# One product of the first block named behind every short matmul of the attention, in the order named

## The chip, the cores and the metric

The program runs on one NeuronCore of a Trainium2 chip (trn2). The metric is the device time of one execution in microseconds (us), lower is better. The engines are named as in the profile: PE is TensorE's matmuls, PEld its weight loads, DVE VectorE, ACT ScalarE, POOL GpSimd, SP SyncE, whose queue issues DMAs.

## The reference: attention and two blocks

All tensors are f32. Attention: batch 4, 8 heads, 576 positions, head dimension 64, with a mask by blocks of 64. Its output becomes 2304 tokens of 512 values. The first block is `h = max(x@w1, x@w2, x@w3)` (width 768), then `h@w_out` (back to 512). The second block is a sum over four experts: `p[:, e] * (relu(x@w1[e]) @ w2[e])`, width 1024.

```python
scores = scale * np.matmul(q, k.transpose(0, 1, 3, 2))      # masked, softmax, then @ v
h = np.maximum(np.maximum(x @ w1, x @ w2), x @ w3); x = h @ w_out
for e in range(E):
    out += p[:, e:e + 1] * (np.maximum(x @ w1[e], 0.0) @ w2[e])
```

## The kernel before

Precision. Most products run on operands split into a high and a low half (`fp32r`), three matmuls for one f32 product (`mm3`, L544 to 554: high with high, high with low, low with high).

Attention (L611 on) goes head by head, g = 0 to 31, eight heads a batch, two heads a pair. The stages of one head are `turn_probs` (transposes of the probabilities on PE, L323, in banks of four tiles, copied out by ACT at L338 and DVE at L339), `values` (products with v, L396 and L404) and `scores` for the head after next (L254, then DVE's minimum, ACT's exponential at L275). On odd heads the next pair is prepared as well (`prep_pair`; `turn_raw` transposes q and k, L199; the DMAs of L158 and L159 copy q to q on ACT's queue). An odd head takes the stages in the order ta, s0, tb, s1, prep, va, prep, vb; an even one in the order ta, tb, va, vb, s0, s1. The PSUM tiles of all of these come from one pool of four banks (`ps_x`).

The first block of a batch (`moe1`) needs the attention of the whole batch. It is a generator, and so its matmuls (L551: 128 rows by 288 columns) are handed out in bits. One bit is six matmuls, a batch has `UNITS` = 96 of them (576 matmuls). `Filler.upto(n)` hands out bits until n are done. After each stage of heads 8 to 31 the kernel asks for as many as the share of the batch that is through, less `LAG` = 10 bits. So batch 0's block is spread over the attention of batch 1, and so on; that of batch 3 comes after the attention.

```python
at = (g + (n + 1) / len(todo)) / H
filler.upto((at - 1) * UNITS - LAG)
```

Order. The program names instructions in an order; a list scheduler that simulates the engines then writes each engine's queue. Where two instructions don't depend on each other, it may take the one named later first, if its inputs are there sooner. `tc.keep_in_program_order(ins)` forbids that for one instruction: it stays behind the instruction of its engine that was named just before it. It adds no semaphore. In the kernel before, no matmul of attention or of the first block is held so. Each engine then runs its queue strictly in order.

The second block (L839, L901 to 903) runs after all of this and is not touched, except that a bit is now one matmul where its first inputs are made (L924).

Of the kernel before, what the change touches and what calls it, by code (L numbers as in the profile page):

```python
# [11 lines left out]
ALU = mybir.AluOpType  # L12
AX = mybir.AxisListType

LAG = 10

WT = 5

# [1 line left out]
P = 128  # L20
# [5 lines left out]
def program(tc, q, k, v, w1, w2, w3, w_out, probs, e_w1, e_w2, out):  # L26
# [166 lines left out]
    def turn_raw(g, to, half):  # L193

        raw = pairs[g]["raw"]
        for r0, r1 in (((0, 8), (8, 16)), ((16, 18),))[half]:
            t = ps_x.tile([P, 512], F32, name="tq", tag="x")
            for r in range(r0, r1, 2):
                nc.tensor.transpose(  # L199
                    t[:, (r - r0) * 64:(r - r0) * 64 + P], raw[:, r:r + 2].rearrange("p r d -> p (r d)"), ident  # L200
                )
            tv = t.rearrange("x (i h p) -> x i h p", h=2, p=64)
            todo = []
            for odd, own, other in ((0, lo, hi), (1, hi, lo)):
                for n in range(2):
                    rs = [r for r in range(r0 + odd, r1, 2) if r // R == n]
                    if rs:
                        dst = to(n, rs[0] - n * R, rs[-1] - n * R + 1, 2)
                        src = tv[own, (rs[0] - r0) // 2:(rs[-1] - r0) // 2 + 1]
                        todo.append((n, dst[own], dst[other], src))  # L210
            for n, high, low, src in todo:
                nc.scalar.activation(high, src, ACTF.Copy, scale=1.0 if n else -scale)
            for n, high, low, src in todo:
                if n:
                    nc.vector.tensor_tensor(low, src, f(high), op=ALU.subtract)
                    continue
                for h in range(2):
                    nc.vector.scalar_tensor_tensor(
                        low[:, :, h], src[:, :, h], -scale, f(high[:, :, h]), op0=ALU.mult, op1=ALU.subtract
                    )  # L220
# [8 lines left out]
    def scores(g, grp):  # L229
        pair, h = pairs[g // 2], g % 2  # L230
        if grp == 0:
            heads[g] = dict(
                p=[None] * 4,
                mn=ap_.tile([P, 5], F32, name="mn", tag="mn", bufs=3),
                sm=ap_.tile([P, 5], F32, name="sm", tag="sm", bufs=3),
            )
        mn, sm, pt = heads[g]["mn"], heads[g]["sm"], heads[g]["p"]
        c0 = 3 * grp
        sets = []
        for tag, cols, plan in GROUPS[1][h] if grp else GROUPS[0]:  # L240
            st = (ps_x if tag == "x" else ps_c).tile([P, cols], F32, name="st", tag=tag)
            sets.append((st, plan))
            for i, o, w in plan:

                if i == 4:
                    todo = [(QT + 64 * x, x) for x in range(2)]
                else:
                    todo = [(h * QT // 2 + P * i, h)]
                c = 0
                while c < w:  # L250
                    n = min(w - c, 512 - (o + c) % 512)
                    terms = [(part, q0, x) for q0, x in todo for part in ("q1", "q2")]
                    for m, (part, q0, x) in enumerate(terms):
                        nc.tensor.matmul(  # L254
                            out=st[:, o + c:o + c + n], lhsT=pair[part][:, q0:q0 + P],
                            rhs=pair["kk"][:, x, c:c + n], start=m == 0, stop=m == len(terms) - 1,
                        )
                    c += n
        c = c0
        done = []  # L260
        for st, plan in sets:
            for i, o, w in plan:
                if i < 4:
                    nc.vector.memset(st[lo, o + w - 64:o + w], 1e30)
            mine = [(c + n, *x) for n, x in enumerate(plan)]
            c += len(plan)
            for col, i, o, w in mine:
                nc.vector.tensor_reduce(mn[:, col:col + 1], st[:, o:o + w], axis=AX.X, op=ALU.min)  # L268
            for col, i, o, w in mine:
                x = ap_.tile([P, w], F32, name=f"p{i}", tag=f"p{i}", bufs=2 if i == 4 else 3)  # L270
                if i == 4:
                    pair["p4"] = x
                else:
                    pt[i] = x
                nc.scalar.activation(  # L275
                    x, st[:, o:o + w], ACTF.Exp, bias=mn[:, col:col + 1], scale=-1.0,
                    accum_out=sm[:, col:col + 1],
                )
                done.append((col, x))

        def normalise():
            cs = slice(c0, c)
            nc.vector.tensor_scalar(sm[:, cs], sm[:, cs], 1e-9, None, op0=ALU.add)
            nc.vector.reciprocal(sm[:, cs], sm[:, cs])  # L284
            for col, x in done:
                nc.gpsimd.tensor_scalar(x, x, sm[:, col:col + 1], 1.0, op0=ALU.mult, op1=ALU.mult)  # L286

        later.append(normalise)
# [14 lines left out]
    def turn_probs(g, part):  # L303

        hd = heads[g]
        banks = PARTS[part]
        if part == 2:

            e4 = ap_.tile([P, 5, 2, 2, 64], F32R, name="e4", tag="e4", bufs=1)
            pairs[g // 2]["e4"] = e4  # L310
        else:
            w = (1024, 256)[part]
            eh = ap_.tile([P, w], F32 if g < H else F32R, name="eh", tag=f"eh{part}", bufs=1)
            el = None if g < H else ap_.tile([P, w], F32R, name="el", tag=f"el{part}", bufs=1)
            hd["e", part] = (eh, el)
        pt = hd["p"] + [pairs[g // 2]["p4"]]
        for n in banks:
            o = 512 * (n - banks[0])
            tt = ps_x.tile([P, 512], F32, name="tt", tag="x")
            c = 0  # L320
            for j, i in BANKS[n]:
                k0 = S - P if j == 4 else j * P
                nc.tensor.transpose(tt[:, c:c + P], pt[i][:, k0:k0 + P], ident)  # L323
                c += P
            if part == 2:
                j0, j1 = BANKS[n][0][0], BANKS[n][-1][0] + 1
                high, low = (e4[:, j0:j1, :, x] for x in range(2))
                src = tt[:, 0:c].rearrange("x (j h q) -> x j h q", h=2, q=64)
                if g < H:
                    nc.scalar.copy(f(high), src)  # L330
                    continue
                nc.scalar.copy(high, src)
                nc.vector.tensor_tensor(low, src, f(high), op=ALU.subtract)
                continue
            if g < H:
                (nc.scalar.copy if n else nc.vector.tensor_copy)(eh[:, o:o + c], tt[:, 0:c])
                continue
            nc.scalar.copy(eh[:, o:o + c], tt[:, 0:c])  # L338
            nc.vector.tensor_tensor(el[:, o:o + c], tt[:, 0:c], f(eh[:, o:o + c]), op=ALU.subtract)  # L339
        if part == 1 and g % 2 == 0:  # L340
            turn_probs(g, 2)
# [45 lines left out]
    def values(g, part):  # L387
# [4 lines left out]
        if part == 0:  # L392

            hd["pv"] = [ps_x.tile([P, 512], F32, name=f"pv{i}", tag="x") for i in range(2)]
            for n, et in enumerate(hd["e", 0]):
                nc.tensor.matmul(  # L396
                    out=hd["pv"][0][:, 0:P], lhsT=vs[:, h, 0], rhs=et[:, 0:P], start=n == 0, stop=n == 1
                )
        pv = hd["pv"][1]
        todo = [(j, to, et[:, of]) for et in hd["e", part] for j, to, of in products(part)]  # L400
        if part:
            todo += [(j, slice(384, 512), pairs[g // 2]["e4"][:, j, h]) for j in range(5)]
        for n, (j, to, x) in enumerate(todo):
            nc.tensor.matmul(out=pv[:, to], lhsT=vs[:, h, j], rhs=x, start=part == 0 and n == 0, stop=j == 4)  # L404
        if part == 0 and h == 0:
            pairs[g // 2]["xf"] = mp.tile([P, S], F32, name="xf", tag="xf", bufs=4)
        xf = pairs[g // 2]["xf"]
# [138 lines left out]
    def mm3(out_, terms):  # L546
        n = 3 * len(terms)
        m = 0
        for wh, wl, xh, xl in terms:
            for w, x in ((wh, xh), (wh, xl), (wl, xh)):  # L550
                nc.tensor.matmul(out=out_, lhsT=w, rhs=x, start=m == 0, stop=m == n - 1)  # L551
                m += 1
                if m % 6 == 0 and m < n:
                    yield

    UNITS = 3 * NF * 2 * 2 + KD * 2 * 3

    xs = {}

# [42 lines left out]

    class Filler:
        def __init__(self):
            self.work, self.done = [], 0

        def upto(self, n):
            while self.done < n and self.work:
                if next(self.work[0], self) is self:
                    self.work.pop(0)  # L610
                else:  # L611
                    self.done += 1

        def rest(self):
            for w in self.work:
# [305 lines left out]
    ready = weights_in(0, 0)  # L921
    for _ in following:

        filler.upto(filler.done + 8)  # L924
    filler.rest()
    moe.close()
    ps.close()
# [65 lines left out]
```

## Time and profile before

| | |
|---|---|
| median of 3 runs | 1286.29 us (1284.87 to 1287.05) |
| the profiled execution | 1287.62 us |
| its span, first to last instruction | 1285.8 us |
| granted TensorE clock, mean | 0.995 of full |
| PE busy | 1256.2 us (98%) |
| PEld busy | 1172.4 us (91%) |
| DVE / ACT / POOL busy | 881.4 / 542.9 / 601.6 us |

The profiled execution is 1.33 us above the median; the span leaves out 1.8 us around it. A matmul has two lines in the trace: PEld is the load of its stationary operand (128x128), PE is the matmul itself. The ends of matmuls are modelled, so a matmul's own length (290 ns, say) overlaps its neighbours, and what one costs is read from start to start.

### The profile page before, as it was taken

The numbers are of one execution on the slowest core, as the hardware profiler recorded it, in microseconds if no ns is written. First come the engines' busy times: TensorE is split into PE (matmuls) and PEld (weight loads), VectorE is DVE, ScalarE is ACT, GpSimd is POOL, SyncE is SP. The second block draws the span as 40 slices with busy tenths as digits, with TensorE's granted clock in tenths as the row PEclk, the third lists the DMA queues.
The fourth block names the chain that finished last, engine by engine and source line by source line (L and its number), as shares of the span: only waits on it lengthen the run. The fifth ranks groups of instructions, "written<-read, shape, count | busy, mean of one in ns | idle before, by whom it ended". The sixth has DMA issues, their size and how long they took to land.

```text
span 1285.8 us, 20501 instructions
## 1 busy us (share of the span) xinstructions
PE 1256.2 (98%) x7510; PEld 1172.4 (91%) x7510; DVE 881.4 (69%) x1667; ACT 542.9 (42%) x1233; POOL 601.6 (47%) x635
## 2 busy tenths in 40 slices
PE   6989999999999999999999999999999999999998
PEld 5879999999999999998999998999999999999997
DVE  6888888666566452387777777677777677777753
ACT  5886677545544330333333333333333423333321
POOL 4985776444244262354444433344444434444420
PEclk9899999999999999999999999999999999999999
DMA  8776686655444363322222213122222122222211
GB/s 211 206 201 176 188 242 198 162 150 142 137 128 125 113 218 114 99 82 66 66 67 66 71 53 92 55 76 66 74 74 66 42 74 66 66 66 66 66 33 49
DMA packets 143716, 138.63 MB, mean 108 GB/s; under 512 B 64384, under 2 KB 110464, under 8 KB 143616
## 3 DMA queue, kind: packets, MB, share of 16 engines
q1 hardware_dynamic: 141216, 127.99, 33.9%
q10 hardware_dynamic: 2400, 9.34, 3.2%
q8 instruction: 59, 0.97, 0.3%
q14 instruction: 41, 0.34, 0.1%
HBM read 110.66 MB, written 17.30 MB: 100 GB/s over the span
## 4 chain that ended last, share of the span: by engine, by line
PE 85%; DVE 5%; ACT 4%; DMA 4%; issue 1%; POOL 1%; SPq 0%; ACTq 0%; DVEq 0%
PE m L839 26%; PE m L551 21%; PE o L903 10%; PE o L902 10%; PE o L901 10%; PE st L254 3%; PE pv L404 2%; PE tt L323 2%; DMA q<-q 2%; ACT p L275 2%; DVE mn L268 1%; DMA wo<-held 1%; PE tq L199 1%; DMA arena<-in_moe_w 0%; DVE hl L867 0%
## 5 line engine op out<-in xcount | busy, mean ns | idle before, releaser
L551 PE MATMUL m<-xh,wt 128*128 128x288 f32 x1120 | 248.1, 301 | 0.0
L903 PE MATMUL o<-w2h,hl 128*128 128x512 f32 x576 | 224.6, 390 | 2.5 <-DVE hl L867 2.5
L901 PE MATMUL o<-w2h,hh 128*128 128x512 f32 x576 | 224.2, 389 | 0.0
L902 PE MATMUL o<-w2l,hh 128*128 128x512 f32 x576 | 224.1, 389 | 0.0
L551 PEld LDWEIGHTS m<-xh,wt 128*128 128x128 f32 x1120 | 186.2, 188 | 0.6
L867 DVE SCALAR_TENSOR_TENSOR hl<-c,hh 128x384 fp32r<-128x384 f32 x144 | 163.2, 1154 | 33.8 <-ACT hh L866 33.2
L551 PE MATMUL m<-xl,wt 128*128 128x288 f32 x560 | 165.8, 296 | 0.0
L732 POOL TENSOR_TENSOR w2l<-r,w2h 128x512 fp32r<-128x512 f32 x88 | 118.6, 1365 | 85.7 <-ACT w2h L731 82.9
L908 DVE SCALAR_TENSOR_TENSOR arena<-o,pr,arena 128x512 f32<-128x512 f32 x126 | 93.7, 744 | 78.0 <-PE o L903 78.0
L732 POOL TENSOR_TENSOR al<-r,ah 128x512 fp32r<-128x512 f32 x44 | 58.2, 1322 | 184.1 <-ACT ah L731 180.3
L732 POOL TENSOR_TENSOR sl<-s,sh 128x1024 fp32r<-128x1024 f32 x44 | 105.6, 2400 | 77.7 <-ACT sh L731 77.7
L903 PEld LDWEIGHTS o<-w2h,hl 128*128 128x128 f32 x576 | 108.0, 188 | 23.4 <-DVE hl L867 2.9
L866 ACT ACTIVATE hh<-c 128x384 fp32r<-128x384 f32 x144 | 71.2, 519 | 127.4 <-DVE c L861 127.4
L901 PEld LDWEIGHTS o<-w2h,hh 128*128 128x128 f32 x576 | 108.1, 188 | 18.0
L902 PEld LDWEIGHTS o<-w2l,hh 128*128 128x128 f32 x576 | 108.1, 188 | 17.9
L286 POOL TENSOR_SCALAR p<-p,sm 128x128 f32<-128x128 f32 (+2 forms) x144 | 85.9, 612 | 49.4 <-DVE sm L284 34.0
L551 PEld LDWEIGHTS m<-xl,wt 128*128 128x128 f32 x560 | 105.4, 188 | 0.6
L275 ACT ACTIVATE p<-st,mn 128x128 f32<-128x128 f32 (+3 forms) x144 | 78.9, 557 | 38.3 <-DVE mn L268 38.1
L731 ACT CAST ah<-r 128x512 fp32r<-128x512 f32 x44 | 27.3, 620 | 149.2 <-issue 120.2
L551 PE MATMUL m<-hh,wo 128*128 128x288 f32 x384 | 83.5, 300 | 0.2 <-DMA wo<-held 0.2
L589 DVE TENSOR_TENSOR mt<-m,mt 128x288 f32<-128x288 f32 x96 | 43.5, 454 | 58.5 <-PE m L551 50.5
L254 PE MATMUL st<-kk,q 128*128 128x128 f32 (+4 forms) x336 | 71.8, 333 | 5.5 <-DMA q<-q 4.0
(184 smaller groups left out, 2963.0 us busy)
## 6 DMA issues: line engine op xcount, KB each, us to landing
wt<-held SPq DMA_DIRECT2D x54, 512.0 KB, 4.0
r<-in_moe_w SPq DMA_DIRECT2D x44, 512.0 KB, 3.6
r<-in_moe_w SPq DMA_DIRECT2D x88, 256.0 KB, 2.6
arena<-in_moe_w SPq DMA_DIRECT2D x18, 512.0 KB, 4.1
wo<-held SPq DMA_DIRECT2D x12, 768.0 KB, 4.4
held<-wt SPq DMA_DIRECT2D x16, 512.0 KB, 3.4
q<-q ACTq DMA_DIRECT2D x26, 304.0 KB, 4.3
arena<-in_q SPq DMA_DIRECT2D x32, 144.0 KB, 3.3
```

Source lines behind the costliest of these rows:

```text
L254: nc.tensor.matmul(out=st[:, o + c:o + c + n], lhsT=pair[part][:, q0:q0 + P], rhs=pair["kk"][:, x, c:c + n], start=m == 0, stop=m == len(t ...
L275: nc.scalar.activation(x, st[:, o:o + w], ACTF.Exp, bias=mn[:, col:col + 1], scale=-1.0, accum_out=sm[:, col:col + 1],)
L286: nc.gpsimd.tensor_scalar(x, x, sm[:, col:col + 1], 1.0, op0=ALU.mult, op1=ALU.mult)
L551: nc.tensor.matmul(out=out_, lhsT=w, rhs=x, start=m == 0, stop=m == n - 1)
L732: (low or nc.gpsimd).tensor_tensor(dst_l, raw, f(dst_h), op=ALU.subtract)
L839: ins = nc.tensor.matmul(out=m, lhsT=w, rhs=x, start=start and n == 0, stop=stop and n == 3 * KH - 1, skip_group_check=True,)
L866: nc.scalar.activation(h, src, ACTF.Relu)
L867: nc.vector.scalar_tensor_tensor(l, src, 0.0, f(h), op0=ALU.max, op1=ALU.subtract)
L901: nc.tensor.matmul(out=o, lhsT=hh[:, ts], rhs=wh, start=i == 0, stop=False)
L902: nc.tensor.matmul(out=o, lhsT=hh[:, ts], rhs=wl, start=False, stop=False)
L903: nc.tensor.matmul(out=o, lhsT=hl[:, ts], rhs=wh, start=False, stop=i == G - 1)
L908: nc.vector.scalar_tensor_tensor(acc, ov, pr[:, tt, e:e + 1], acc, op0=ALU.mult, op1=ALU.add)
```

## The change

A bit of the first block becomes one matmul. Every matmul of the attention with at most 128 columns goes through `filler.between`: while there is work of the first block, that matmul is kept in the order named, and one matmul of the first block is named right behind it and kept there too. This concerns the transposes of L199 and L323, the products of L396, and those of L254 and L404 with 128 columns. The transposes of `turn_parts` (pairs 0 to 5) are left as they are. The rest of the first block is still handed out after the stages, to the same share of the batch: `LAG` = 60 and `UNITS` = 576 count matmuls now. In heads 0 to 7 there is no work yet, and `between` does nothing.

```diff
-LAG = 10
+LAG = 60
...
-                nc.tensor.transpose(
+                filler.between(nc.tensor.transpose(
                     t[:, (r - r0) * 64:(r - r0) * 64 + P], raw[:, r:r + 2].rearrange("p r d -> p (r d)"), ident
-                )
+                ))
...
-                        nc.tensor.matmul(
+                        ins = nc.tensor.matmul(
...
+                        if n <= P:
+                            filler.between(ins)
...
-                nc.tensor.transpose(tt[:, c:c + P], pt[i][:, k0:k0 + P], ident)
+                filler.between(nc.tensor.transpose(tt[:, c:c + P], pt[i][:, k0:k0 + P], ident))
...
-                nc.tensor.matmul(
+                filler.between(nc.tensor.matmul(
                     out=hd["pv"][0][:, 0:P], lhsT=vs[:, h, 0], rhs=et[:, 0:P], start=n == 0, stop=n == 1
-                )
+                ))
...
-            nc.tensor.matmul(out=pv[:, to], lhsT=vs[:, h, j], rhs=x, start=part == 0 and n == 0, stop=j == 4)
+            ins = nc.tensor.matmul(
+                out=pv[:, to], lhsT=vs[:, h, j], rhs=x, start=part == 0 and n == 0, stop=j == 4
+            )
+            if to.stop - to.start <= P:
+                filler.between(ins)
...
-                nc.tensor.matmul(out=out_, lhsT=w, rhs=x, start=m == 0, stop=m == n - 1)
+                ins = nc.tensor.matmul(out=out_, lhsT=w, rhs=x, start=m == 0, stop=m == n - 1)
+                if filler.here:
+                    tc.keep_in_program_order(ins)
                 m += 1
-                if m % 6 == 0 and m < n:
+                if m < n:
                     yield
 
-    UNITS = 3 * NF * 2 * 2 + KD * 2 * 3
+    UNITS = 3 * NF * 2 * 3 * KD + KD * 2 * 3 * NF
...
+        def between(self, ins):
+
+            if not self.work:
+                return
+            tc.keep_in_program_order(ins)
+            self.here = True
+            self.upto(self.done + 1)
+            self.here = False
...
-        filler.upto(filler.done + 8)
+        filler.upto(filler.done + 48)
```

## Rows read from the trace of the kernel before

**Rows 1.** The page: busy time of the engines over the span, and the granted clock in 40 slices.

```profile
PE 1256.2 (98%) x7510; PEld 1172.4 (91%) x7510; DVE 881.4 (69%) x1667; ACT 542.9 (42%) x1233; POOL 601.6 (47%) x635
...
PEclk9899999999999999999999999999999999999999
```

**Rows 2.** Busy time of each engine by stretch: start and end in us, length, then busy us and number of instructions of PE, PEld, DVE, ACT, POOL, the granted clock, the DMA engines' share and GB/s. First the two heads in which the first block begins, then the rest of the attention of batches 1 to 3, then a stretch with the first block alone.

```profile
94.00:120.00 26.00, 24.37 (x184) 23.73 (x183) 20.23 (x55) 19.33 (x53) 13.37 (x22) 1.00 0.50 149
120.00:440.00 320.00, 316.93 (x2422) 314.26 (x2422) 227.32 (x625) 181.93 (x482) 164.27 (x261) 1.00 0.58 163
480.00:520.00 40.00, 40.00 (x304) 40.00 (x303) 7.32 (x16) 3.20 (x8) 9.90 (x16) 1.00 0.33 98
```

**Rows 3.** What PE waited for between 93 and 450 us: engine and line, what ended the wait, us in total, times, longest.

```profile
PE st L254 <- DMA q<-q: 4.0, 4, 1.3
PE st L254 <- ACT p L275: 0.5, 1, 0.5
PE m L551 <- DMA wo<-held: 0.2, 1, 0.2
```

**Rows 4.** The same stretches as in group 2, the first block's matmuls (L551) alone: PE and PEld, clock, DMA.

```profile
94.00:120.00 26.00, 16.07 (x108) 14.76 (x108) 1.00 0.50 149
480.00:520.00 40.00, 40.00 (x304) 40.00 (x303) 1.00 0.33 98
```

**Rows 5.** Groups by line between 93.9 and 445 us: three kinds of short matmul. Count, busy us, mean ns of one, idle before.

```profile
L199 PE MATMUL tq<-ident,arena 128*128 128x128 f32 x90 | 14.2, 272 | 0.0
L323 PE MATMUL tt<-ident,p 128*128 128x128 f32 x299 | 47.1, 272 | 0.0
L404 PE MATMUL pv<-e,vs 128*128 128x128 f32 x115 | 16.6, 261 | 0.0
```

**Rows 6.** Timeline of PE around 185 us: start, us from the first start to the last end of the instructions merged in the line, what, count. Four transposes, one matmul of the first block, one transpose, then the first block again.

```profile
184.94 0.60 PE L323 MATMUL tt<-ident,p 128*128 128x128 f32 x4
185.29 0.38 PE L551 MATMUL m<-xh,wt 128*128 128x288 f32 x1
185.51 0.27 PE L323 MATMUL tt<-ident,p 128*128 128x128 f32 x1
185.54 0.38 PE L551 MATMUL m<-xh,wt 128*128 128x288 f32 x1
185.75 0.30 PE L551 MATMUL m<-xl,wt 128*128 128x288 f32 x1
```

**Rows 7.** The weight loads of the same place.

```profile
185.26 0.19 PEld L551 LDWEIGHTS m<-xh,wt 128*128 128x128 f32 x1
185.40 0.14 PEld L323 LDWEIGHTS tt<-ident,p 128*128 128x128 f32 x1
185.51 0.19 PEld L551 LDWEIGHTS m<-xh,wt 128*128 128x128 f32 x1
185.62 0.19 PEld L551 LDWEIGHTS m<-xl,wt 128*128 128x128 f32 x1
```

**Rows 8.** Timeline of PE around 221 us: products of 128 columns (L404) among matmuls of the first block.

```profile
221.00 0.45 PE L404 MATMUL pv<-e,vs 128*128 128x128 f32 x3
221.28 0.35 PE L551 MATMUL m<-hh,wo 128*128 128x288 f32 x1
221.46 0.22 PE L404 MATMUL pv<-e,vs 128*128 128x128 f32 x1
221.52 0.35 PE L551 MATMUL m<-hh,wo 128*128 128x288 f32 x1
221.71 0.29 PE L551 MATMUL m<-hl,wo 128*128 128x288 f32 x1
```

**Rows 9.** Timeline of PE around 148 us: two products of 128 columns, the second started while its own load was still under way.

```profile
148.23 0.22 PE L396 MATMUL pv<-eh,vs 128*128 128x128 f32 x1
148.29 0.27 PE L396 MATMUL pv<-el,vs 128*128 128x128 f32 x1
```

**Rows 10.** Timeline of PE: the first and the last run of short matmuls next to the first block's (641 short matmuls in 230 runs lie between 93.8 and 445 us).

```profile
93.81 0.38 PE L323 MATMUL tt<-ident,p 128*128 128x128 f32 x2
...
439.27 0.22 PE L396 MATMUL pv<-eh,vs 128*128 128x128 f32 x1
```

**Rows 11.** Timeline of ACT and DVE where the first block begins: the last quarter of batch 0's attention output is split into its halves.

```profile
95.30 0.70 ACT L569 CAST xh<-xf 128x576 fp32r<-128x576 f32 x1
...
96.03 1.19 DVE L570 TENSOR_TENSOR xl<-xf,xh 128x576 fp32r<-128x576 f32 x1 [1.79 <-ACT xh L569]
```

**Rows 12.** Timeline of an even head around 304 us: transposes of ta, their copies by ACT and DVE, transposes of tb, first product of va.

```profile
304.14 0.60 PE L323 MATMUL tt<-ident,p 128*128 128x128 f32 x4
304.28 1.09 ACT L338 CAST eh<-tt 128x512 fp32r<-128x512 f32 x2
304.90 1.29 DVE L339 TENSOR_TENSOR el<-tt,eh 128x512 fp32r<-128x512 f32 x2
...
307.20 0.60 PE L323 MATMUL tt<-ident,p 128*128 128x128 f32 x4
...
308.03 0.27 PE L323 MATMUL tt<-ident,p 128*128 128x128 f32 x1
...
308.54 0.22 PE L396 MATMUL pv<-eh,vs 128*128 128x128 f32 x1
```

More of the change, by code (lines that the diff above doesn't have):

```diff
@@ L604, in __init__ @@
         def __init__(self):
-            self.work, self.done = [], 0
+            self.work, self.done, self.here = [], 0, False
         def upto(self, n):
```

## The prediction

> **What bounds the kernel now.** I read the page first: PE is busy for 98% of the span, its weight loads for 91%, no other engine beyond 69%, and the clock is at its upper level (2.4 GHz) after the first slices [rows 1]. Then the stretches: in the attention of batches 1 to 3, which is where the change acts, PE idles 1.63 us of the first 26 and 3.07 us of the next 320 [rows 2]. The list of waits says that 4.0 of these 4.7 us are four waits of a score product for the copy of q, 0.5 one wait for ACT [rows 3]. So two questions decide: does a short matmul cost less with a long one behind it, and does the fixed order open gaps? Closing gaps can give at most 4.7 us.
>
> **The price of a matmul.** Where the first block runs alone, 304 matmuls of 288 columns fill 40.00 us [rows 2, 4]: 0.1316 us each, say L. A short one, S: four transposes in a row last 0.60 us and a single one 0.27 [rows 6], so three spacings take 0.33 us and S is 0.110. Streaming alone would be shorter: two products of 128 columns start 0.06 us apart when the second's load is late [rows 9]. What S pays for, then, is the load of the matmul behind it: successive loads start 0.11 us apart (185.40, 185.51, 185.62) [rows 7], and none starts before the matmul ahead of its own has begun (both at 185.51) [rows 6, 7]. L covers the load behind it, S doesn't.
>
> **The change on PE.** By the code there are 650 such S in heads 8 to 31: 90 in preparing pairs, 300 transposes of probabilities, 44 in scores, 216 in values; the trace has 90 and 299 of the first two, and 115 of the 120 of one kind in values [rows 5]. The change removes no matmul and adds none; it alternates S L S L where there were runs of S. The kernel before already does that in places, by the scheduler's choice. From the four S at 184.94 over L, S, L to the next L at 185.75 are 0.81 us [rows 6]; five S and two L add up to 5 x 0.110 + 2 x 0.1316 = 0.813. From three S at 221.00 over L, S, L to 221.71 are 0.71 [rows 8]; four S and two L make 0.703. The S between two L costs its full 0.110. The reason is the one above: the load of the L behind S starts only when S starts, whatever stood before S. **So alternating gains 0.** It may cost a little: the first of these places lies 0.003 under its sum, the second 0.007 over it with two runs of S: 0 to 4 ns a run. There were 230 runs for 641 recorded S [rows 10]; there will be up to 650, some 420 more: 0 to 1.7 us. I take 1, between the two places.
>
> The Trainium skill (TensorE: Matmul & The Clock Gate, Part 2: What happens when you issue a matmul) says that PE pulls weight loads ahead of matmuls in flight when they go to the background weight buffer; read as a deep look-ahead, it speaks for the change. The trace shows one load ahead and no more [rows 6, 7]. That reading is the second rival; its price stands there, worked out from rows.
>
> **Where the first block begins (heads 8 and 9).** Before, 108 of its matmuls ran in these 26 us [rows 4]. After, 26 are pinned behind the short matmuls of head 8 (15 transposes, 9 values, 2 scores); the pace asks for 84 by the end of head 9 (2 x 72 less 60), and what is named later mostly can't be drawn forward, because every sum of 12 now holds pinned members. Without their 108 x 0.1316 = 14.2 us and without idle time the two heads hold 10.2 us of PE work; with 84 it is 21.2 us, against 20.2 us of DVE and 19.3 of ACT [rows 2]. PE loses most of its slack over DVE: the 24 missing matmuls, 3.2 us, are the cover that is gone. Also, the tenth matmul needs the last quarter of its input, whose low half DVE finishes at 96.03 + 1.19 = 97.22 [rows 11]; the first eight pairs S L (0.242 each) from 93.8 end at 95.7 [rows 10], so up to 1.2 us of waiting, in front of which the pinned transposes of tb then stand. Upper bound 4.4 us, lower bound a gain of the 1.63 us that PE idles there now. I take 1.5: long score products aren't pinned and can still fill.
>
> **The later heads.** A pinned transpose or product that waits for its input now holds back the first block's matmul behind it, and all pinned ones after that; before, the scheduler put others in front. What covers this: in an even head, va needs DVE's low halves of ta's banks. The last four transposes start at 304.14, the last of them at 304.14 + 0.33 = 304.47, DVE is done at 304.90 + 1.29 = 306.19, and va starts at 308.54 [rows 12]. After, by the order named, between ta's last transpose and va stand 16 L and 7 S (4 L at the end of ta's share of 12, then tb's 7 S with 7 L and 5 more): 16 x 0.1316 + 7 x 0.110 = 2.9 us, against 306.19 - 304.47 = 1.7 us needed. The cover holds with 1.2 us to spare, and I cost it at 0; if copies come later than that by a queue on DVE, the excess is paid in each of 24 heads. DVE is busy 71% of these 320 us [rows 2], so some heads will pay. Bounds: 3.07 us gained (all gaps gone) and 0.3 us a head lost, 22 x 0.3 = 6.6, an estimate from a quarter of the spare time; I take 1, near the 3.07 us that such waits cost now over all heads. The waits for q's copy I leave where they are: the copies move with the stages that name them. The work of DVE, ACT, POOL and the DMAs is the same, as are the two banks of the first block and its pace; converting and loading its weights is named at the same matmul as before, with 24 matmuls between two tiles, so I cost that at 0. After the attention, 60 matmuls and batch 3's block remain, as before: 0.
>
> **Sum.** 0 + 1 + 1.5 + 1 = 3.5 us on the profiled execution's 1287.62 us, hence 1291.1; that execution is 1.33 above the median, so **1289.8 us** for the median.
>
> **The rivals.**
> (a) The fixed order costs much: pinned transposes that wait for one of the four PSUM banks. In tb of an even head three banks are wanted soon after ta's two. Before, the scheduler held the last bank's transpose back to 308.03, 0.83 us after the four at 307.20, with three L ahead of it [rows 12]. After, four pairs S L take 0.97 us to the same point, so alternating spaces the demand for banks by itself; that speaks against. For it speaks that nothing else may go first when a bank is late. It decides from about 0.1 us a head (24 x 0.1 = 2.4); at 0.5 us a head it is 12 us, about 1299 to 1305.
> (b) Loads are hidden after all. If several loads could run ahead, a pair would cost two loads, 0.220, in place of 0.242: 650 x 0.022 = 14 us, 1272. If S cost its stream of 0.06 alone: 650 x 0.05 = 32 us, 1254. For it: such long alternation, tens of pairs, isn't in the trace. Against it: the two places above [rows 6 to 8].
> (c) Faster through gaps: the new order delays the score products that wait for q's copy, and PE's 4.7 us shrink to 1 or less with nothing new: 1286.3 - 4 = 1282.3. For it: more matmuls now stand ahead of them in the same stage. Against it: PE has only these few gaps, and every pin takes freedom away. A half of it, with the cost of alternating, is no change.
> (d) Naming an order doesn't set neighbours: unpinned long products may slip between S and L. As S costs 0.110 anywhere, that moves nothing: 1286 to 1288.
>
> **How the numbers follow.** A measurement of this kernel tells about 0.2% (2.6 us) from no change. The forecast's case, small costs with its bounds, 1285 to 1295, has 0.57, of which 0.17 lies within 0.2% of 1286.3, below 1288.9. (a), 1295 to 1305, has 0.17. (b) has 0.05, (c) 0.09, of which 0.03 stays within 0.2%, (d) 0.12, all within 0.2%. Faster: 0.05 + 0.06 = 0.11. Same: 0.17 + 0.03 + 0.12 = 0.32. Slower: 0.40 + 0.17 = 0.57. The range that leaves out (b), the far half of (a) and the best of (c) is 1283 to 1300.
>
> **What would show it.** Right: single transposes between single matmuls of the first block, with pairs 0.24 us apart; PE's idle time between 94 and 440 us above 4.7, most of the increase before 120 us; waits of transposes or L551 for DVE or ACT new in the list. Wrong: pairs of S and L at 0.19 to 0.22 us would mean that loads hide, and the price of S was misread; a sum of waits near 12 us would mean (a); a list of waits without q's copy (c).

## The result, and the profile after

The changed kernel takes **1295.35 us** (median of 4 runs, 1292.88 to 1297.24) against 1286.67 (4 runs of the kernel before on the same chip): ratio **1.0062**, interval 1.0048 to 1.0077, 8.7 us slower by the medians. A second set of 6 runs gave 1295.41 and 1.0073 [1.0053, 1.0093]. The forecast was slower, 1289.8 us, in a range of 1283 to 1300: right in sign, and the size fell short by 5.5 us. The profiled execution was the quickest of the first four (1292.88 us, span 1291.0), so the profile shows 5.3 of the 8.7 us.

The page of the changed kernel, to set beside [rows 1]: work and clock look alike.

```profile
PE 1261.1 (98%) x7510; PEld 1174.4 (91%) x7510; DVE 888.4 (69%) x1667; ACT 544.7 (42%) x1233; POOL 597.7 (46%) x635
...
PEclk9999999999999999999999999999999999999999
```

The stretches of [rows 2]. Columns as there. In the first 26 us PE now idles 4.86 us (1.63 before), in the next 320 us 2.01 (3.07 before).

```profile
94.00:120.00 26.00, 21.14 (x154) 19.79 (x152) 20.93 (x60) 17.70 (x46) 12.23 (x19) 1.00 0.52 143
120.00:440.00 320.00, 317.99 (x2406) 313.06 (x2405) 226.71 (x614) 179.84 (x476) 156.22 (x258) 1.00 0.56 161
```

The first block alone, from its first matmul (at 91.27 us) to 120 us: 84 matmuls in 28.7 us. Before, 108 ran from the first one (93.95 us) to 120 us, in 26.0 us [rows 4].

```profile
91.20:120.00 28.80, 18.95 (x84) 14.27 (x84) 1.00 0.56 152
```

What PE waits for between 93 and 450 us, for [rows 3]. The waits for q's copy fell from 4.0 to 1.5 us; waits for ACT's exponential (L277, L275 before), other than one of a score product, and for DVE are new.

```profile
PE st L254 <- DMA q<-q: 1.5, 2, 1.1
PE tt L325 <- ACT p L277: 1.5, 1, 1.5
PE pv L406 <- ACT p L277: 0.9, 2, 0.7
PE pv L398 <- ACT p L277: 0.8, 1, 0.8
PE m L557 <- DVE xl L578: 0.7, 1, 0.7
PE m L557 <- DMA wo<-held: 0.6, 1, 0.6
```

The timeline of PE in head 8, for [rows 6]: the alternation is there.

```profile
91.74 0.27 PE L325 MATMUL tt<-ident,p 128*128 128x128 f32 x1
91.76 0.38 PE L557 MATMUL m<-xh,wt 128*128 128x288 f32 x1
91.98 0.27 PE L325 MATMUL tt<-ident,p 128*128 128x128 f32 x1
92.01 0.39 PE L557 MATMUL m<-xh,wt 128*128 128x288 f32 x1
92.23 0.27 PE L325 MATMUL tt<-ident,p 128*128 128x128 f32 x1
```

From transpose to transpose is 0.24 to 0.25 us, the sum 0.110 + 0.1316 and a little more. Nothing of the load is hidden. In the whole trace 649 short matmuls stand in 640 runs (230 before).

**Where the time went.** Three marks in PE's timeline split the stretch: the first matmul of the first block, its 577th (batch 0's block is through), and the first of the second block. The kernel before:

```profile
93.95 0.38 PE L551 MATMUL m<-xh,wt 128*128 128x288 f32 x1
...
225.23 0.29 PE L551 MATMUL m<-xh,wt 128*128 128x288 f32 x1
...
534.26 0.33 PE L839 MATMUL m<-b11h,ah 128*128 128x384 f32 x1
```

The changed kernel:

```profile
91.27 0.38 PE L557 MATMUL m<-xh,wt 128*128 128x288 f32 x1
...
228.70 0.29 PE L557 MATMUL m<-xh,wt 128*128 128x288 f32 x1
...
538.75 0.33 PE L856 MATMUL m<-b11h,ah 128*128 128x384 f32 x1
```

Part A, batch 0's block, grew from 131.3 to 137.4 us; part B, the rest, from 309.0 to 310.0. By the code, the change does nothing before the first mark; that stretch differs from profile to profile (90.0 to 95.6 us over all kernels here) and is left out below.

### The profile page after: what moved, and what is told of

It reads as the page before. It is cut to its first block, busy times and chain, and to the rows that moved or that the text cites. A ratio compares the mean times of both kernels' runs of the same rounds, so it can differ in the third digit from the quotient of the medians.

```text
span 1291.0 us, 20514 instructions
## 1 busy us (share of the span) xinstructions
PE 1261.1 (98%) x7510; PEld 1174.4 (91%) x7510; DVE 888.4 (69%) x1667; ACT 544.7 (42%) x1233; POOL 597.7 (46%) x635
## 4 chain that ended last, share of the span: by engine, by line
PE 89%; DVE 5%; ACT 3%; DMA 2%; issue 1%; POOL 0%; SPq 0%; ACTq 0%; DVEq 0%
PE m L856 26%; PE m L557 23%; PE o L920 10%; PE o L919 10%; PE o L918 10%; PE st L254 3%; PE tt L325 2%; PE pv L406 2%; ACT p L277 1%; DMA q<-q 1%; DVE mn L270 1%; PE tq L199 1%; PE tq L180 1%; DVE sm L285 0%; DMA wo<-held 0%
## 5 line engine op out<-in xcount | busy, mean ns | idle before, releaser
L557 PE MATMUL m<-xh,wt 128*128 128x288 f32 x1120 | 269.2, 315 | 0.0
L557 PEld LDWEIGHTS m<-xh,wt 128*128 128x128 f32 x1120 | 192.5, 189 | 2.5 <-DVE mt L597 1.4
L557 PE MATMUL m<-xl,wt 128*128 128x288 f32 x560 | 178.2, 318 | 0.7 <-DVE xl L578 0.7
L925 DVE SCALAR_TENSOR_TENSOR arena<-o,pr,arena 128x512 f32<-128x512 f32 x126 | 93.8, 744 | 77.0 <-PE o L920 77.0
L325 PE MATMUL tt<-ident,p 128*128 128x128 f32 x400 | 92.8, 277 | 4.4 <-ACT p L277 2.2
L277 ACT ACTIVATE p<-st,mn 128x128 f32<-128x128 f32 (+4 forms) x144 | 78.7, 557 | 28.8 <-DVE mn L270 28.4
L557 PE MATMUL m<-hh,wo 128*128 128x288 f32 x384 | 88.7, 310 | 1.0 <-DMA wo<-held 0.6
L254 PE MATMUL st<-kk,q 128*128 128x128 f32 (+4 forms) x336 | 76.2, 324 | 2.8 <-DMA q<-q 1.5
```

The costliest lines, as they stand in the source:

```text
L254: ins = nc.tensor.matmul(out=st[:, o + c:o + c + n], lhsT=pair[part][:, q0:q0 + P], rhs=pair["kk"][:, x, c:c + n], start=m == 0, stop=m == ...
L277: nc.scalar.activation(x, st[:, o:o + w], ACTF.Exp, bias=mn[:, col:col + 1], scale=-1.0, accum_out=sm[:, col:col + 1],)
L325: filler.between(nc.tensor.transpose(tt[:, c:c + P], pt[i][:, k0:k0 + P], ident))
L557: ins = nc.tensor.matmul(out=out_, lhsT=w, rhs=x, start=m == 0, stop=m == n - 1)
L925: nc.vector.scalar_tensor_tensor(acc, ov, pr[:, tt, e:e + 1], acc, op0=ALU.mult, op1=ALU.add)
```

## The experiments

Ten further kernels (e1 to e10) and a second profile of each of the two. Each profile but that of e4, which computes nothing of the program, was split at the same three marks. Parts are in us; matmuls of attention may stand on either side of the middle mark, so their sum is the safer number.

| kernel | A | B | A + B | median us | ratio to before |
|---|---|---|---|---|---|
| before, two profiles | 131.3, 129.8 | 309.0, 309.6 | 440.3, 439.4 | 1286.67 | 1 |
| changed, two profiles | 137.4, 139.0 | 310.0, 310.3 | 447.5, 449.3 | 1295.35, 1295.41 | 1.0062, 1.0073 |
| e1 finer bits alone | 130.7 | 307.0 | 437.8 | 1283.68 | 0.9982 [0.9971, 0.9992] |
| e5 named, nothing pinned | 131.1 | 307.4 | 438.5 | 1283.81 | 0.9982 [0.9969, 0.9995] |
| e6 short ones pinned, none named | 132.4 | 307.1 | 439.4 | 1285.61 | 0.9996 [0.9982, 1.0009] |
| e10 products pinned alone | 137.3 | 306.4 | 443.7 | 1293.3 | 1.0053 [1.0034, 1.0072] |
| e3 heads 8 and 9 alone | 139.4 | 305.8 | 445.2 | 1291.31 | 1.0038 [1.0025, 1.0051] |
| e2 from head 10 | 137.1 | 309.6 | 446.7 | 1294.43 | 1.0063 [1.0051, 1.0075] |
| e8 from head 16 | 134.8 | 310.2 | 445.0 | 1290.56 | 1.003 [1.002, 1.004] |
| e9 from head 18 | 132.4 | 309.7 | 442.0 | 1286.17 | 1.0008 [0.9995, 1.002] |
| e7 more named early | 139.1 | 309.9 | 449.0 | 1295.51 | 1.007 [1.005, 1.009] |

**The price of a short matmul (e4).** TensorE alone, operands in place, each matmul kept in order, loads from four places of one tile:

```python
pattern("longs", "L", 64); pattern("shorts", "S", 64); pattern("pairs", "SL", 64)
pattern("twos", "SSLL", 32); pattern("turns", "T", 64); pattern("turnpairs", "TL", 64)
pattern("wide", "H", 64); pattern("widepairs", "SH", 64); pattern("threes", "SLL", 43)
pattern("blocks", "SSSSSSSSLLLLLLLL", 8)
```

> None of the reference is computed; zeros are written out. TensorE alone runs patterns, all in the order named, with operands in place: S = product of 128 columns, T = transpose, L = 288 columns, H = 512. If one load goes ahead and no more, a matmul costs the larger of its stream and the load behind it, wherever it stands: L 132 ns, S 110, T 109, a pair S L 242, S S L L 483, T L 241, H 231, S H 341, S L L 373, eight S and eight L 1933. If alternating itself costs: S L 246 to 248, blocks of eight near 1937. If loads can run further ahead: S L 220. If S is wholly hidden: S L 192, S H 291.

The first matmul of each pattern, from PE's timeline:

```profile
28.04 0.29 PE L50 MATMUL longsl<-r 128*128 128x288 f32 x1
...
36.47 0.22 PE L50 MATMUL shortss<-r 128*128 128x128 f32 x1
...
43.56 0.28 PE L50 MATMUL pairss<-r 128*128 128x128 f32 x1
...
59.19 0.22 PE L50 MATMUL twoss<-r 128*128 128x128 f32 x1
...
74.70 0.27 PE L46 MATMUL turnss<-ident,raw 128*128 128x128 f32 x1
...
81.68 0.27 PE L46 MATMUL turnpairss<-ident,raw 128*128 128x128 f32 x1
...
97.36 0.40 PE L50 MATMUL widel<-r 128*128 128x512 f32 x1
...
111.89 0.22 PE L50 MATMUL widepairss<-r 128*128 128x128 f32 x1
...
133.66 0.22 PE L50 MATMUL threess<-r 128*128 128x128 f32 x1
...
149.86 0.22 PE L50 MATMUL blockss<-r 128*128 128x128 f32 x1
...
165.44 0.29 PE L50 MATMUL endl<-r 128*128 128x288 f32 x1
```

From start to start by the count: L (36.47 - 28.04) / 64 = 131.7 ns, S 110.8, T 109.1. The pair S L takes 15.63 / 64 = 244.2 (the sum is 242.5), S S L L 484.7 (485.0), the pair T L 245.0 (240.8). Even 512 columns hide nothing: H 227.0, S H 340 (337.8). So one load goes ahead and no more; a matmul costs the larger of its own stream and the load behind it, wherever it stands. Alternating costs 2 ns a pair with products, 4 with transposes. The last two patterns lie further above their sums than was expected: S L L 376.7 (374.2), eight S and eight L 1947.5 (1940.0). Eight pairs S L would take 1953.6, only 6 ns more than such a block, so an order in blocks saves less than 1 ns a pair. This settles rival (b).

**Which part of the change costs (e1, e5, e6, e10).** e1 leaves the finer bits and takes out the rest; e5 names without pinning; e6 pins the short matmul and names nothing; e10 pins the first block's matmul and not the short one:

```diff
 def between(self, ins):          # e1
-    if not self.work:
-        return
+    return
 def between(self, ins):          # e5
-    tc.keep_in_program_order(ins)
-    self.here = True
+    self.here = False
     self.upto(self.done + 1)
 def between(self, ins):          # e6
     tc.keep_in_program_order(ins)
-    self.here = True
-    self.upto(self.done + 1)
-    self.here = False
 def between(self, ins):          # e10
-    tc.keep_in_program_order(ins)
     self.here = True
```

> The changed kernel with nothing named behind the short matmuls and nothing pinned; what is left of the change is that a bit of the first block is one matmul and not six (LAG 60, UNITS 576). If the pins and the alternation cost the time: 1286 to 1288 us, PE idle 4 to 5 us between 93 and 450 us, some 230 runs of short matmuls. If the finer bits cost it: 1293 us or more.

> The changed kernel with one matmul of the first block named behind every short one, but nothing pinned: the scheduler may move all. The finer bits alone gave 1283.7 us, the changed kernel 1295.4. If the pins make the difference: 1284 to 1287 us, gaps before 120 us as in the kernel before. If naming and alternating make it: 1291 us or more.

> The changed kernel with the short matmuls pinned and nothing named behind them; the first block's matmuls come after the stages alone and are free. If what hurts is that the first block's matmuls can't be drawn forward into gaps: 1284 to 1287 us, few gaps. If it is the fixed order of the short ones themselves: 1290 us or more, with waits for ACT at 105 to 120 us as in the changed kernel.

> The changed kernel with the first block's matmul pinned behind the short one, and the short one not pinned. With neither pinned 1283.8 us, with the short ones alone pinned 1285.6, with both 1295.4. If the pinned product is what hurts, since it takes the first block's matmuls from the scheduler as filling: 1290 to 1295 us. If it takes both pins: 1284 to 1287 us.

e1 did better than either line said: 1283.68 us, quicker than the kernel before. So the change holds a small gain, and the rest of it costs 11.7 us, not 8.7. Its marks:

```profile
91.02 0.38 PE L557 MATMUL m<-xh,wt 128*128 128x288 f32 x1
...
221.77 0.30 PE L557 MATMUL m<-xh,wt 128*128 128x288 f32 x1
...
528.81 0.33 PE L855 MATMUL m<-b11h,ah 128*128 128x384 f32 x1
```

e5 is the same within its interval: with nothing pinned the scheduler put most products elsewhere (285 runs of short matmuls). e6 lies between e1 and the kernel before. e10 brings back most of the loss. The list of waits of e6, 88 to 450 us, and under it that of e10:

```profile
PE st L254 <- DMA q<-q: 3.2, 2, 1.7
PE m L557 <- DVE wo L504: 0.6, 1, 0.6
PE st L254 <- ACT p L277: 0.5, 1, 0.5
```

```profile
PE tt L325 <- ACT p L277: 1.5, 1, 1.5
PE pv L398 <- ACT p L277: 0.8, 1, 0.8
...
PE pv L406 <- ACT p L277: 0.7, 1, 0.7
```

The waits of 1.5, 0.8 and 0.7 us for ACT that the changed kernel has are here with the short matmuls free, and not with them pinned. What takes PE's cover is the pin on the first block's matmuls. With it alone all that is lost between the marks is in part A; part B is as short as in e1.

**Where it costs (e2, e3, e7, e8, e9).** e2, e8 and e9 let `between` act from head 10, 16 and 18 on (`self.head < 10: return`), e3 in heads 8 and 9 alone; e7 drops LAG for four heads:

```diff
-            filler.upto((at - 1) * UNITS - LAG)
+            filler.upto((at - 1) * UNITS - (0 if g < H + 4 else LAG))
```

> The changed kernel, but naming and pinning begin with head 10, not 8. If most of the loss is that the first block's matmuls can't be drawn forward in heads 8 and 9: gaps of 2 us or less before 120 us, and 1288 to 1290 us, what is left being 4 to 5 ns for each of some 350 more runs of short matmuls. If the pins cost alike in every head: 1294 us (22 of 24 heads keep them).

> The changed kernel, but naming and pinning only in heads 8 and 9 (some 56 short matmuls). If those two heads make most of the loss: gaps of 4 to 5 us between 91 and 120 us as in the changed kernel, 1291 to 1293 us, none new later. If the loss is spread over the heads: 1287 to 1288 us.

> The changed kernel with LAG 0 in heads 8 to 11 in place of 60, so that the program names 60 matmuls of the first block more by the end of head 9, in front of the later pinned ones. If the loss at the start is missing cover: the gaps of 3 us at 105 to 115 us go, and 1288 to 1291 us. If the pinned matmuls wait for PSUM banks whatever is named ahead: gaps as before, 1294 to 1296 us.

> The changed kernel with naming and pinning from head 16 on only, where the first block's work is plentiful and DVE less busy. Alternating at 4 to 7 ns for each of some 280 more runs of short matmuls is 1 to 2 us on the 1283.7 us of the finer bits: 1285 to 1286 us. If pins cost wherever they begin: gaps of some us after 205 us and 1289 us or more.

> The changed kernel with naming and pinning from head 18 on only, when batch 0's block, whose weights ACT, POOL and DVE prepare during heads 8 to 16, is through. If the pins hurt because a matmul waits for engines that are full in that stretch: only alternating is left, 4 to 7 ns for each of some 240 more runs of short matmuls, 1284.5 to 1286 us. If pins cost wherever they begin: 1288 us or more.

e3 came out as the first theory said: two heads of pins cost 7.6 us against e1 and bring the gaps back; not expected were two waits of 0.3 us for ACT at 181 and 183 us. e2 missed: without the pins of heads 8 and 9 hardly anything is won, A stays at 137.1 us. The pins of head 10 bar what is named from there on just as well, so heads 8 and 9 still have only the 84 matmuls named for them (84 run in the 26 us behind its first mark, 108 in e1). e7 missed as well, and tells most: with 60 more named early the gaps before 120 us went, but for 0.8 us of waiting for `xl`, and as many came back, at 159 to 191 us, when LAG had returned at head 12. From its list of waits, 88 to 450 us, three that are at 178 to 191 us:

```profile
PE pv L398 <- ACT p L277: 1.2, 1, 1.2
PE tq L199 <- DVE el L341: 1.0, 1, 1.0
...
PE tt L325 <- DVE last L428: 0.8, 1, 0.8
```

So most gaps stand where fewer first-block matmuls are named than before, whichever heads these are. e8 shows another wait at head 16: a matmul of the first block waited for its own weights, the last of batch 0's, which DVE was still making. Whether the pins made this wait is not shown: e6, where the first block's matmuls are free, has 0.6 us of it. The line of e8:

```profile
PE m L557 <- DVE wo L504: 1.1, 1, 1.1
```

e9 begins when batch 0's block is nearly through, and its loss is nearly gone: 1286.17 us, and from the first mark on PE's list has no wait for ACT or DVE that the kernel before doesn't have. Its last two marks:

```profile
227.74 0.30 PE L557 MATMUL m<-xh,wt 128*128 128x288 f32 x1
...
537.40 0.33 PE L857 MATMUL m<-b11h,ah 128*128 128x384 f32 x1
```

Part B is 309.7 us, 2.6 more than in e1 with the same matmuls. Two waits for weights are new in it (0.24 and 0.50 us in the list, at 333 and 533 us; 0.40 and 0.66 from start to start, beyond the price of the matmul in front). Another 0.8 us lies in waits that PE's own list doesn't show, because the modelled ends of matmuls cover them. The list of the weight loads (PEld) from 229 to 530 us has four waits of 0.2 us for DVE's L597, which reads a PSUM bank of the first block. The changed kernel has five. So does every kernel with both pins in part B, four or five, while the kernel before, e1, and e6 and e10 with one pin each have none of these. The changed kernel's line, and the first of its five places on PE:

```profile
PEld m L557 <- DVE mt L597: 0.9, 5, 0.2
```

```profile
242.88 0.31 PE L254 MATMUL st<-kk,q 128*128 128x320 f32 x1
243.13 0.40 PE L557 MATMUL m<-xh,wt 128*128 128x288 f32 x1
243.37 0.29 PE L557 MATMUL m<-xl,wt 128*128 128x288 f32 x1
```

From 242.88 to 243.37 are 0.49 us, where a score product of 320 columns (0.14, in a row of four at 247.75 us) and an L make 0.27: 0.2 us lost at each place. That leaves 2.6 - 1.1 - 0.8 = 0.7 us over 455 - 221 = 234 more runs of short matmuls, 3 ns a run. That is the price of alternating in this kernel, as in e4 (2 to 4 ns) and in the prediction (0 to 4).

**Second profiles (e11, e12).**

> The kernel before, a second look. From the first matmul of the first block to the second block 440 us, of which waits for the copy of q 3 to 4 us; 1285 to 1288 us. If the 3 us that the finer bits won came out of those waits, this look shows them as the first did.

> The changed kernel, a second look. 1293 to 1297 us, gaps of about 5 us before 120 us again; if the gaps let the clock fall, the granted clock is 0.5 in some us near 110 to 120 us, which the first look did not show.

e11, the kernel before: 439.4 us between the marks, waits for q's copy 2.5 us, fewer than expected, but one of 1.11 us at 271 us as in the first profile (1.27 at 276). In all ten kernels with finer bits there is none after 220 us. With the waits for weights (0.2 and 0.7 us in the two profiles) it makes most of the 2.0 and 2.6 us by which e1's part B is shorter. e12, the changed kernel, has the same gaps again, and shows what the first profile didn't: behind the waits at 96.2 (0.74 us, for DVE) and 98.7 (1.07, for q's copy) the clock fell. The stretch from 98 to 104 us, with the granted clock behind POOL's busy time, in e12 and then in the first profile:

```profile
98.00:104.00 6.00, 5.35 (x29) 5.38 (x30) 2.12 (x6) 0.90 (x3) 1.28 (x1) 0.72 0.29 87
```

```profile
98.00:104.00 6.00, 6.00 (x48) 5.92 (x46) 2.37 (x9) 2.43 (x5) 1.28 (x1) 1.00 0.28 87
```

In e12 PE ran more than half of these 6 us at its lower level, 1.2 GHz, and part A took 1.6 us longer than in the first profile. e2 and e3 show the same at 119 to 120 us and e8 at 212 us, each just behind new gaps; both profiles of the kernel before and those of e1, e5, e6, e7, e9 and e10 have the full clock from 80 to 530 us, e7 and e10 with new gaps too.

## Why the prediction was right, and which terms were off

**The price of S: right.** Forecast 0 from alternating, measured 0 gained: pairs of 0.24 to 0.25 us in the changed kernel, 244 and 245 ns in e4. The Trainium skill (TensorE: Matmul & The Clock Gate, Part 2: What happens when you issue a matmul) speaks of weight loads pulled ahead of matmuls in flight; the runs agree for one load, the one behind the running matmul, and exclude the deep look-ahead of rival (b).

**The alternation: right.** 1 us forecast from 420 more runs at 0 to 4 ns. Measured 3 ns a run in part B of e9, which for the changed kernel's 419 more runs than e1's is an estimated 1.3 us.

**Where the first block begins: the mechanism right, the size not.** The step named the 24 missing matmuls as the cover that is gone, with the last quarter's low half late by up to 1.2 us. Both are there: 84 matmuls in place of 108 before 120 us, and a wait of 0.7 us for `xl`. It was priced at 1.5 us with 4.4 as upper bound. The 30 us behind the first mark, in e1 and then in the changed kernel:

```profile
91.02:121.02 30.00, 28.28 (x215) 27.64 (x214) 23.97 (x64) 20.89 (x57) 16.80 (x27) 1.00 0.56 161
```

```profile
91.27:121.27 30.00, 25.14 (x185) 23.71 (x184) 23.10 (x62) 21.17 (x56) 16.06 (x26) 1.00 0.57 154
```

PE idles 1.72 us and 4.86: 3.1 more. The modelled ends hide some 0.2 us in each gap, as is worked out below, and there are five gaps against two, so the loss is an estimated 3.7 us: more than twice the price, and within the bound. (The 7.6 us of e3 hold more than this term: in its profiled execution the clock fell too, and two waits came later.) I expected unpinned score products to fill; they did not. In the changed kernel's timeline the pinned pairs stop at a transpose, and what comes next on PE is that transpose:

```profile
104.14 0.27 PE L325 MATMUL tt<-ident,p 128*128 128x128 f32 x1
104.17 0.38 PE L557 MATMUL m<-xh,wt 128*128 128x288 f32 x1
106.02 0.33 PE L325 MATMUL tt<-ident,p 128*128 128x128 f32 x1 [1.48 <-ACT p L277]
```

The transpose waits for ACT's exponential, whose end frees the PSUM bank of a score tile (that it is the bank is inferred from the pool, not seen). Before, the scheduler laid 21 matmuls of the first block, from 106.24 us on, ahead of eight such transposes at 109.02. So rival (a)'s wait for banks seems to have occurred, but only at 106 to 115 and 206 to 209 us and not in every head: it is the same loss of cover. By its time alone, 1295.35 us, the result lies at the near end of what the prediction gave to (a), 1295 to 1305, and just outside its own case, 1285 to 1295. That the range of 1283 to 1300 holds it is owed to the room left for (a). The waits of PE's list sum to 6.8 us (4.7 before), short of the 12 that the prediction named as the sign of (a). From 104.17 to 106.02 are 1.85 us, of which 0.13 is the price of the matmul: 1.72 lost, where the list says 1.48. Matmul ends are modelled, and each of the dozen gaps hides some 0.2 us so. The clock behind the gaps, 1.6 us in e12, was not in the sum at all.

**The later heads: too small.** 1 us was forecast. Between 179 and 222 us, the end of batch 0's block, PE waits four times for DVE or ACT, 0.18 to 0.31 us, 1.0 us together by the list; later its list has no such wait, and va's cover held there. In part B come two waits for weights (0.55 and 0.45 us in the list, at 334 and 534 us; 1.3 from start to start) and the five for the first block's own PSUM banks, 1.0 us. The prediction had costed the weights, and with them the two banks and the pace, at 0.

**The finer bits: a term that was missing.** I costed the smaller bit at nothing without a row for it, and left the waits for q's copy where they were. e1 measures a gain of 2.3 us by its ratio (1.0 to 3.7), most of it q copies and weights that no longer are late in part B.

By the profiles, against e1: 447.5 - 437.8 = 9.7 us more between the marks in the first profile, 6.7 in A and 3.0 in B. In B, 1.3 are the waits for weights and 1.0 those for the first block's banks; 0.7 are left for the 255 more runs, 3 ns each as in e9. In A the alternation is an estimated 0.5 (164 more runs) and the start of the first block 3.7; the other 2.5, the waits from 179 us on among them, were not split further. The medians differ by 11.7; e12, 1.9 us longer than the first profile between the marks, 1.6 of it in the part with the fallen clock, shows where part of the rest comes from. How often the clock falls so was not counted.

Left open: whether a pace without LAG through all heads, with the weights of batch 0 made earlier, would take the cover loss away. It was not run. The best version is e1, the finer bits alone, 0.2% under the kernel before; e5 is level with it.

## What to carry to other kernels

Before interleaving short matmuls with long ones to hide weight loads, read two places of the trace where a short one already stands alone between long ones: the loss a short matmul brings is the load behind it, and that load can't start before the short one does, so order doesn't help. Work that fills gaps is worth its freedom: pin the work that has to be in order, not the filler, and give the filler out in fine bits. When a pinned order shows gaps, ask where filler is named too late rather than which head has the gap; in e7 the gap moved with the naming.

## What the runs showed of the hardware that was not expected

Transposes kept the full clock: 64 in a row in e4, 74.70 to 81.68 us, ran at 109 ns each with a granted clock of 1.00, and short matmuls of either kind cost the same 109 to 111 ns. In four profiles with new gaps (e12, e2, e3, e8) the granted clock fell to 1.2 GHz just behind waits of 0.7 to 1.5 us in dense work; in three (e7, e10 and the first profile of the changed kernel, which has the gaps of e12 in the same places) it did not, and what decides was not found. PE's list of waits is not complete: waits of 0.2 us that stand in the list of its weight loads cost 0.2 us each from start to start and do not appear on PE.
